# Nine loads that nobody reads, ahead of the first K tile of a decode attention kernel

## The chip, the cores and the metric

The kernel runs on one core of one Trainium2 chip. The metric is the device time of one execution in microseconds. Before the change the median of two runs is 1277.88 us (1277.71 to 1278.06).

## The reference

One token (a row `x` of 448 numbers) passes through two branches, which a gate mixes:

```
g = sigmoid(sum(x * gate_w))
q = x @ wq                                   # 16 heads of 256, two to a K/V head
p = softmax(q . k_cache / 16)                # 8 K/V heads, 65536 positions each
a = (p @ v_cache) @ wo                       # 4096 -> 448
b = (relu(x @ W_gate) * (x @ W_up)) @ W_down # 448 -> 1792 -> 448
out = g * a + (1 - g) * b
```

All inputs are bf16. The two caches, 8 x 65536 x 256 each, are nearly all of the data: 537 MB of the 549 MB that the kernel reads.

## The kernel before

**Tiles.** Each K/V head is cut into four tiles of 16384 positions (`NTH = 4`), 32 tiles of K and 32 of V. A tile is a `[128, 32768]` bf16 buffer: 128 partitions with 64 KB each. For K, a partition's 64 KB lie 256 KB after those of the partition before it in memory (`k_src`), for V 64 KB (`v_src`). There are three such buffers, `ring[0]` to `ring[2]`, which K and V tiles, and at the end the last pieces of V and `wo`, use in turn.

**What happens to a tile.** VectorE transposes a K tile in place in 32 x 32 blocks (L373, in two halves for the first head), TensorE forms the scores of both query heads (L388, L414), VectorE joins the two score banks and takes the maximum (L559, L561), ScalarE exponentiates (L563). After a head's fourth K tile VectorE rescales and transposes the probabilities (L580, L582), and TensorE multiplies them with the V tiles (L461, L414). A buffer is free again when TensorE has read it.

**Who issues the loads.** The list `order` names the loads in the order in which SyncE issues them, with due times; each operation carries a key (its due time), and each engine runs its operations in the order of their keys. SyncE issues nearly everything: first the main part of `wq` (key 3.0, into `ring[2]`), then `W_up` (3.002), the rest of `wq` (`wqa`, 3.01, into the first columns of `ring[1]`), K tile 0 (into `ring[0]`), eight small loads of 5 or 3 partitions that bring the last 64 rows of `W_gate` and `W_up` (`rows64`, L399), `W_down` (L539, which waits until `q` is formed, since it overwrites `wq`), K tile 1 (into `ring[1]`), K tiles 2 and 3, and from there V and K by turns. ScalarE issues `W_gate`, `x` and `gate_w` at the start. GpSimd issues no load before the change; it clears a part of `ring[2]` first (L257), for which `rows64` waits, and then makes identity matrices and selectors.

**When a tile's load may start.** `slot` gives each tile its buffer, `freed` what must be done with that buffer before, and `held` starts this record with what stands in the buffers at the beginning: `q` in buffer 1, the gate/up products and the down product in buffer 2. A name in it stands for the operation or the load of that name in `l_`, and `free()` turns it into a wait of the tile's load. The wait is made on a count: a DMA's semaphore has its full count when all its parts have landed.

**The end.** The last V tile comes in three pieces (L603), with pieces of `wo` (L618) behind them; two copies (L656) and a small store (L658) end the program.

Of the kernel before, what the change touches and what calls it, by code (L numbers as in the profile page):

```python
# [24 lines left out]
class _Plan:  # L25
# [13 lines left out]
    def dma(self, eng, key, sem, fn, deps=()):  # L39
        if sem not in self.dsem:  # L40
            self.dsem[sem] = self.es.enter_context(self.nc.semaphore("d_" + sem))
        o = _Op(eng, key, fn, deps, dma=sem)
        self.ops.append(o)
        return o
# [59 lines left out]
def bass_gated_mix__gqa_block_cached__glu_gated_reglu__decode_kernel(  # L104
# [39 lines left out]
    with es:  # L144
# [3 lines left out]
        ring = [sb("ring%d" % i, [128, U * DH], BF) for i in range(NRING)]  # L148
# [59 lines left out]
        op, dma = pl.op, pl.dma  # L208
# [30 lines left out]
        T_END = t + 20.0  # L239


        slot, held, freed = {}, {1: ["q"], 2: ["gu", "dn"]}, {}
        r = 0
        for kind, i, _ in order:
            if kind in ("k", "v") or (kind, i) in (("wo", 0), ("vp", 0)):
# [158 lines left out]
        l_, qk, smax, aexp, pv, last = {}, {}, {}, {}, {}, {}  # L404
# [83 lines left out]
        for kind, i, t in issue:  # L488
            if kind == "wq":
                l_["wq"] = dma("sp", t, "wq", lambda e: e.dma_start(wq3, A_wq[0:NR3, :].rearrange("(p k) n -> p (k n)", k=R3)))  # L490
                l_["wqh"] = dma("sp", t + 0.01, "wqh", lambda e: e.dma_start(
                    wqa, A_wq[NR3:D, :].rearrange("r (c n) -> (r c) n", c=2)))
                tq = tL["wq", 0]
# [54 lines left out]
            elif kind == "k":  # L548
                n = i
# [45 lines left out]
            elif kind in ("v", "vp"):  # L595
                if kind == "v":
                    n, lo, hi = i, 0, U
# [99 lines left out]
```

## Time and profile before

| | before |
|---|---|
| median of the runs | 1277.88 us (2 runs, 1277.71 to 1278.06) |
| the profiled execution | 1277.58 us |
| its span in the profile | 1276.3 us |
| busy: VectorE, TensorE, ScalarE, GpSimd | 685.0, 352.4, 51.2, 10.6 us |
| bytes moved by DMA | 549.46 MB, 431 GB/s over the span |
| SyncE's queue (with ScalarE's first loads in another) | 99.4% of 16 engines' span |

The span runs from the first to the last instruction of the profile; the profiled execution's own time is 1.28 us longer. Engines' busy times overlap, so they do not add up to the span. In the views of stretches each row gives a stretch of the span, its length, the busy time (and number) of each engine's instructions in it, TensorE's granted clock, the mean busy share of the 16 DMA engines and the rate. In the views of waits a row says which queue and line waited for what: us in total, times, longest. In the view of DMA issues the last number is the median time from issue to landing, where it is known. In a timeline a row begins with its start and its length in us.

### The profile page before, as it was taken

The numbers are of one execution on the slowest core, as the hardware profiler recorded it, in microseconds if no ns is written. First come the engines' busy times: TensorE is split into PE (matmuls) and PEld (weight loads), VectorE is DVE, ScalarE is ACT, GpSimd is POOL, SyncE is SP. The second block draws the span as 40 slices with busy tenths as digits, with TensorE's granted clock in tenths as the row PEclk, the third lists the DMA queues.
The fourth block names the chain that finished last, engine by engine and source line by source line (L and its number), as shares of the span: only waits on it lengthen the run. The fifth ranks groups of instructions, "written<-read, shape, count | busy, mean of one in ns | idle before, by whom it ended". The sixth has DMA issues, their size and how long they took to land.

```text
span 1276.3 us, 6848 instructions
## 1 busy us (share of the span) xinstructions
PE 352.4 (28%) x4447; PEld 70.6 (6%) x1875; DVE 685.0 (54%) x283; ACT 51.2 (4%) x84; POOL 10.6 (1%) x23
## 2 busy tenths in 40 slices
PE   3322323213122240133320242211323203223135
PEld 2000000000000000000000000000000000000001
DVE  2688733576534755445555454556535566336521
ACT  0000000000000000000000000000000000000000
POOL 3000000000000000000000000000000000000000
PEclk9556666665666565666655666656766556666567
DMA  9999999999999999999999999999999999999998
GB/s 403 439 434 429 440 430 429 438 431 434 433 426 444 433 428 433 430 442 430 428 438 431 430 435 430 432 440 433 430 432 432 440 431 430 432 435 440 426 421 368
DMA packets 11594, 549.46 MB, mean 431 GB/s; under 512 B 1287, under 2 KB 1418, under 8 KB 2570
## 3 DMA queue, kind: packets, MB, share of 16 engines
q1 hardware_dynamic: 11418, 547.66, 99.4%
q10 hardware_dynamic: 148, 1.38, 0.3%
q8 instruction: 24, 0.39, 0.1%
q14 instruction: 4, 0.03, 0.0%
HBM read 549.03 MB, written 0.00 MB: 430 GB/s over the span
## 4 chain that ended last, share of the span: by engine, by line
DVE 40%; DMA 28%; PE 17%; another core or an unknown queue 11%; ACT 1%; issue 1%; SPq 0%; ACTq 0%; DVEq 0%
DVE ring L373 32%; DMA ring<-in_A_k_cache_dram 24%; PE ST L388 5%; PE ST L414 5%; PE O L414 4%; DMA ring<-in_A_wo_dram 3%; PE O L461 2%; DVE o_sb L423 2%; DVE P L582 1%; DVE P L580 1%; ACT P L563 1%; DMA P<-in_A_x_dram 1%; DVE nmb L561 1%; DVE ST L559 1%
## 5 line engine op out<-in xcount | busy, mean ns | idle before, releaser
L373 DVE STREAM_TRANSPOSE ring<-ring 128x16384 uint32<-128x16384 uint32 (+1 forms) x36 | 552.3, 15346 | 311.6 <-DMA ring<-in_A_k_cache_dram 307.2
L388 PE MATMUL ST<-ring,xm 128*16 128x512 bf16 x1024 | 140.1, 539 | 772.5 <-DVE ring L373 772.5
L414 PE MATMUL ST<-ring,xm 128*16 128x512 bf16 x1024 | 137.1, 527 | 0.0
L414 PE MATMUL O<-ring,P 128*32 128x512 bf16 x1524 | 118.6, 423 | 0.0
L559 DVE COPY_PREDICATED ST<-bm,ST 128x512 f32<-128x512 uint16 x32 | 22.2, 694 | 168.7 <-PE ST L414 168.7
L563 ACT ACTIVATE P<-ST,nmb 128x512 bf16<-128x512 f32 x32 | 45.3, 1415 | 1135.8 <-DVE nmb L561 1135.8
L388 PEld LDWEIGHTS ST<-ring,xm 128*16 128x16 bf16 x1024 | 31.8, 115 | 929.1 <-DVE ring L373 801.1
L461 PE MATMUL O<-ring,P 128*32 128x512 bf16 (+1 forms) x524 | 56.3, 427 | 23.6 <-DMA ring<-in_A_v_cache_dram 23.5
L423 DVE CAST_PREDICATED o_sb<-bm,O 128x512 bf16<-128x512 uint16 (+1 forms) x33 | 22.3, 679 | 62.1 <-PE O L414 58.8
L580 DVE TENSOR_TENSOR P<-P,hs 128x2048 bf16<-128x2048 bf16 x8 | 18.3, 2293 | 8.5 <-ACT hs L577 8.5
L561 DVE TENSOR_REDUCE nmb<-ST 128x1 f32<-128x512 f32 x32 | 22.1, 691 | 1.1
L461 PEld LDWEIGHTS O<-ring,P 128*32 128x32 bf16 (+1 forms) x524 | 15.9, 113 | 119.8 <-issue 91.4
L582 DVE STREAM_TRANSPOSE P<-P 128x2048 bf16<-128x2048 bf16 x8 | 18.5, 2311 | 0.3
L587 PE MATMUL M_ps<-hs,ones_f 128*128 128x2 f32 x16 | 4.7, 363 | 46.0 <-DVE hs L586 46.0
L441 PE MATMUL M_ps<-emat,o_sb 128*128 128x2 bf16 x72 | 3.3, 167 | 23.6 <-DVE o_sb L433 23.2
L563 ACT ACTIVATION_READ_ACCUMULATOR P<-ST,nmb 128x1 f32 x32 | 8.5, 266 | 0.0
L339 PE MATMUL M_ps<-ring,P 128*128 128x256 bf16 x48 | 7.1, 321 | 0.3 <-DVE gb L295 0.3
L308 DVE COPY xm<-P 1x64 bf16<-1x64 bf16 x2 | 0.3, 190 | 12.2 <-DMA P<-in_A_x_dram 12.2
L587 PEld LDWEIGHTS M_ps<-hs,ones_f 128*128 128x128 f32 x16 | 4.0, 312 | 46.7 <-DVE hs L586 46.7
L573 PE MATMUL M_ps<-identf,hs 128*2 128x128 f32 x8 | 2.2, 270 | 15.8 <-DVE hs L571 15.8
L257 POOL MEMSET ring<- 64x7168 bf16 x1 | 6.1, 6064 | 0.3 <-POOLq L682 0.3
L481 DVE TENSOR_SCALAR attnT<-M_ps,hs 64x4 bf16<-64x4 f32 x16 | 3.5, 220 | 3.8 <-PE M_ps L441 3.7
(89 smaller groups left out, 79.8 us busy)
## 6 DMA issues: line engine op xcount, KB each, us to landing
ring<-in_A_v_cache_dram SPq DMA_DIRECT2D x1, 4096.0 KB, 29.8
ring<-in_A_v_cache_dram SPq DMA_DIRECT2D x2, 2048.0 KB, 36.5
ring<-in_A_wq_dram SPq DMA_DIRECT2D x1, 3072.0 KB, 13.2
ring<-in_A_wo_dram SPq DMA_DIRECT2D x4, 448.0 KB, 39.6
ring<-in_B_W_down_dram SPq DMA_DIRECT2D x1, 1568.0 KB, 17.1
ring<-in_B_W_gate_dram ACTq DMA_DIRECT2D x1, 1344.0 KB, 13.5
ring<-in_B_W_up_dram SPq DMA_DIRECT2D x1, 1344.0 KB, 16.0
ring<-in_A_wo_dram SPq DMA_DIRECT2D x1, 1344.0 KB, 18.7
```

The costliest lines, as they stand in the source:

```text
L339: ins = e.matmul(QN_ps, xw3[:, kt, 31 - j:159 - j], wq3[:, kt * NQ + j * 256:kt * NQ + (j + 1) * 256], start=(j == 0 and kt == 0), stop=Fa ...
L373: return lambda e: e.transpose(v, v)
L388: ins = e.matmul(o, xm[:, x0:x0 + 16], v, start=st, stop=False, skip_group_check=True, tile_position=(0, 32 * w))
L414: return e.add_instruction(mybir.InstMatmult(name=nc.get_next_instruction_name(), engine=e.engine, ins=[e.lower_ap(v), e.lower_ap(w, for_m ...
L423: return e.copy_predicated(dst, m.to_broadcast(list(src.shape)), src)
L461: ins = e.matmul(o, w, v, start=st, stop=False, skip_group_check=True, tile_position=(0, 32 * g))
L559: join = op("dv", tk + 25.2, lambda e: e.copy_predicated(ST[0][:], bm[:, NB:NB + 1].bitcast(mybir.dt.uint16).to_broadcast([128, 512]), ST[ ...
L561: smax[n] = op("dv", tk + 26, lambda e, n=n, NM=NM, t_=t_: e.tensor_reduce(NM[:, t_:t_ + 1], ST[0][:], AX.X, ALU.max, negate=True), [join, ...
L563: aexp[n] = op("ac", tk + 27, lambda e, n=n, t_=t_, NM=NM, RS=RS, Ph=Ph: e.activation(Ph[:, t_:2048:4], ST[0][:], ACTF.Exp, bias=NM[:, t_: ...
L580: rsc = op("dv", T + 16, lambda e, X=X, pb=pb: e.tensor_tensor(pb, pb, X[:, 12:16].unsqueeze(1).to_broadcast([128, 512, 4]), ALU.mult), [h ...
L582: last["ev", h] = [op("dv", T + 17, lambda e, Ph=Ph: e.transpose(Ph[:], Ph[:]), [rsc])]
L587: l3 = mop("pe", T + 19, lambda e, X=X: e.matmul(LS_ps, ones_f[:, :], X[:, 6:8], start=True, stop=True), [l2, c_one])
```

## The change

Nine loads of parts of `wq` are added, into columns of `ring[1]` (the buffer of K tile 1) that hold nothing else at that time. No instruction reads what they bring. Seven are issued by SyncE, with keys just behind the weights' and ahead of K tile 0's: load `i` takes `27 + 3 i` rows of `wq`, three rows (24 KB) to a partition, to the `9 + i` partitions `i`, `i + 8`, `i + 16`, ... Two are issued by GpSimd ahead of everything else that it does: four partitions each, 24 KB to a partition, 0, 8, 16, 24 and 32, 40, 48, 56. K tile 1, which overwrites the buffer, waits for them too. On the other engines no instruction is added, removed or moved.

```diff
-        slot, held, freed = {}, {1: ["q"], 2: ["gu", "dn"]}, {}
+        slot, held, freed = {}, {1: ["q", "pk", "pg"], 2: ["gu", "dn"]}, {}
...
                 l_["wq"] = dma("sp", t, "wq", lambda e: e.dma_start(wq3, A_wq[0:NR3, :].rearrange("(p k) n -> p (k n)", k=R3)))
+                for i in range(7):
+                    l_["pk"] = dma("sp", 3.02 + 0.001 * i, "pk", lambda e, i=i: e.dma_start(
+                        ring[1][i:i + 8 * i + 65:8, 8192:20480], A_wq[0:3 * i + 27, :].rearrange("(p k) n -> p (k n)", k=3)))
+                for i in range(2):
+                    l_["pg"] = dma("gp", -0.9 + 0.01 * i, "pg", lambda e, i=i: e.dma_start(
+                        ring[1][i * 32:i * 32 + 25:8, 20480:32768], A_wq[12 * i:12 * i + 12, :].rearrange("(p k) n -> p (k n)", k=3)))
                 l_["wqh"] = dma("sp", t + 0.01, "wqh", lambda e: e.dma_start(
                     wqa, A_wq[NR3:D, :].rearrange("r (c n) -> (r c) n", c=2)))
```

## The prediction

> **What bounds the kernel now.** I read the page's header first, then the busy time by stretches of the span, then the waits of SyncE's queue.
>
> ```profile
> span 1276.3 us, 6848 instructions
> DMA packets 11594, 549.46 MB, mean 431 GB/s; under 512 B 1287, under 2 KB 1418, under 8 KB 2570
> core 0: us, PE busy (x) PEld busy (x) DVE busy (x) ACT busy (x) POOL busy (x), PEclk, DMA share, GB/s
> 64.31:103.00 38.69, 6.64 (x68) 1.10 (x32) 35.67 (x8) 2.79 (x4) 0.00 (x0) 0.57 1.00 434
> 200.00:400.00 200.00, 57.05 (x765) 9.48 (x285) 104.22 (x35) 9.00 (x14) 0.00 (x0) 0.63 1.00 433
> 400.00:800.00 400.00, 103.02 (x1319) 18.75 (x519) 214.64 (x81) 15.56 (x26) 0.00 (x0) 0.63 1.00 433
> 1200.00:1240.00 40.00, 17.27 (x221) 4.16 (x93) 12.95 (x14) 1.85 (x4) 0.00 (x0) 0.67 0.97 413
> ```
>
> From 200 to 800 us the sixteen DMA engines are busy all the time (share 1.00) and move 433 GB/s, while VectorE is busy about half and TensorE a quarter. One engine thus moves 433 / 16 = 27.06 GB/s. All bytes at that rate take 549.46 / 0.433 = 1269.0 us, against the execution's 1277.58: the transfers set the time, and only 8.6 us, at the two ends, is not theirs. That is also all that any edit that removes no bytes could win at this rate.
>
> ```profile
> SPq L599 <- PE ST L414: 905.8, 29, 36.1
> SPq L552 <- PE O L414: 165.0, 27, 15.4
> ring<-in_A_k_cache_dram SPq DMA_DIRECT2D x32, 50.4
> ring<-in_A_v_cache_dram SPq DMA_DIRECT2D x31, 35.0
> ```
>
> SyncE waits nearly always for a free ring buffer, but ahead of need. A tile is 128 x 64 KB = 8.39 MB, or 19.4 us at 433 GB/s; a K tile lands 50.4 us and a V tile 35.0 us after its issue (medians), so 31 and 15.6 us of other work lie queued ahead of them. Late issues start to cost only once these are used up.
>
> **Few partitions, few engines.** Whether a load of 9 partitions is shared by all engines decides its price, and before has such loads: L399 brings eight of 5 or 3 partitions, between the first K tile and W_down.
>
> ```profile
> ring<-in_B_W_gate_dram SPq DMA_DIRECT2D x2, 70.0 KB
> ring<-in_B_W_gate_dram SPq DMA_DIRECT2D x1, 52.5 KB
> ring<-in_B_W_gate_dram SPq DMA_DIRECT2D x1, 31.5 KB
> ring<-in_B_W_up_dram SPq DMA_DIRECT2D x2, 70.0 KB
> ring<-in_B_W_up_dram SPq DMA_DIRECT2D x1, 52.5 KB
> ring<-in_B_W_up_dram SPq DMA_DIRECT2D x1, 31.5 KB
> ring<-in_B_W_down_dram SPq DMA_DIRECT2D x1, 1568.0 KB, 17.1
> 37.85 8.71 DVE L373 STREAM_TRANSPOSE ring<-ring 128x8192 uint32<-128x8192 uint32 x1 [7.32 <-DMA ring<-in_A_k_cache_dram]
> 41.29 1.67 PE L526 MATMUL O<-ring,xT 20*1 20x448 bf16 x32 [11.53 <-DMA ring<-in_B_W_up_dram]
> 28.22 36.09 DMA ring<-in_A_k_cache_dram
> ```
>
> K tile 0 releases VectorE at 37.85; K tile 1 (the last row, from the chain of waits: issued at 28.22) lands 36.09 us later, at 64.31. In these 26.46 us lie the tile (19.37 us), W_down (1.606 MB, 3.71 us) and the eight loads, gate and up, 448 KB in all. What remains for these is 26.46 - 23.08 = 3.38 us. Spread over 16 engines they would take 0.459 MB / 433 GB/s = 1.06 us. On as many engines as partitions, the fullest engine has 2 x (14 + 14 + 10.5 + 10.5) = 98 KB, 3.71 us at 27.06 GB/s. The measured 3.38 us lies there, and it was paid in full by the next tile: a lag of a few engines holds up everybody, because a tile is complete with its last engine. So I count the new loads by their fullest engine.
>
> **The change, part by part.** It removes nothing. It adds nine DMA issues and, for K tile 1, a wait for them.
>
> *Seven loads of SyncE*, 9 to 15 partitions, 24 KB each, queued behind the weights and ahead of K tile 0. Load i has 9 + i partitions; if each goes to one engine, counted from the first, nine engines get seven packets each, the tenth six, the sixteenth none. A packet is 24,576 B / 27.06 GB/s = 0.908 us. Lower bound: each engine at full rate, 7 x 0.908 = 6.36 us. Upper bound: here the destination partitions step by eight (0, 8, ... 64 in the first), while L399's step by four (0, 4, ... 16). [...] I take the upper end, since the rows nearest to the limit show no part of the reading side: K tiles alone, whose rows lie 256 KB apart, come at 434 GB/s (64.31 to 103.00), K and V by turns, V's rows 64 KB apart, at 433. What is read does not set the rate, and where it is written may.
>
> [...]
>
> *Two loads of GpSimd*, 4 partitions each (0, 8, 16, 24 and 32, 40, 48, 56), at the start, beside the weights. One packet on an engine is 0.91 us; if both loads end in the same four sets, 1.82 us. No row shows a GpSimd load. I take the middle, 1.3 us; a gain is excluded because all engines are loaded at that time:
>
> ```profile
> 0.00:20.00 20.00, 2.22 (x18) 1.70 (x19) 4.93 (x25) 1.49 (x2) 10.64 (x23) 1.00 0.97 400
> 0.73 6.06 POOL L257 MEMSET ring<- 64x7168 bf16 x1 [0.29 <-POOLq L682]
> 1.65 0.43 SPq L491 DMA_DIRECT2D ring<-in_A_wq_dram  x1
> 2.12 0.54 SPq L552 DMA_DIRECT2D ring<-in_A_k_cache_dram  x1
> 6.82 3.01 SPq L399 DMA_DIRECT2D ring<-in_B_W_gate_dram  x4
> 9.87 2.85 SPq L399 DMA_DIRECT2D ring<-in_B_W_up_dram  x4
> 20.72 0.16 DVE L322 TENSOR_REDUCE emat<-identb 128x4 bf16<-128x64 bf16 x1
> 27.82 0.35 SPq L539 DMA_DIRECT2D ring<-in_B_W_down_dram  x1
> ring<-in_A_wq_dram SPq DMA_DIRECT2D x1, 512.0 KB, 16.8
> ```
>
> *Issue time: 0 us.* Seven more issues at 0.54 to 0.75 us (3.01 / 4) push K tile 0's issue from 2.12 to about 6 or 7.5 us, under weights that land until about 18.4 (the second part of wq: issued at 1.65, 16.8 us to landing). GpSimd's two issues stand before the 6.06 us memset for which L399 waits; from 0.4 to 3 us each, they move it to at most 13 and L399's last issue to about 19, with K tile 0 in the queue until 37.85 or later; identb, which VectorE reads at 20.72, also stays ahead. Without that cover they would cost 6 us.
>
> *The new wait: 0 us.* K tile 1 writes over the padding, so SyncE now waits for it: 18.4 + 14.0 = 32.4 us instead of 28.22. Behind it in SyncE's queue stand K tiles 2 and 3, which wait for later things. K tile 0, by then landing at about 51.9, hides these 4 us; they would be paid only if it did not.
>
> *What is late next.* K tile 0 lands 14 us later and so does every tile behind it, on the loaded engines; VectorE, TensorE and the ring follow their last engine, so the depth of 15.6 us is the same for that engine. The others run ahead and idle, which costs nothing.
>
> Sum: 12.7 + 1.3 = 14.0 us. 1277.58 + 14.0 = 1291.6 for the profiled execution; the median of the runs is 0.3 above it, which gives **1291.9 us**, 1.1% slower.
>
> **The rivals.**
>
> *Engines at full rate, no sharing:* 6.36 + 0.91 = 7.3 us, 1285.2. For it: L399's loads ran at full rate. Against it: their partitions do not collide.
>
> *Spread or hidden:* over all engines 92 packets of 24,576 B are 2.26 MB / 433 GB/s = 5.2 us, 1283.1; if the engines with the loads are not the ones that end last, down to 0, 1277.9. Against it the 3.38 us above.
>
> *Not slower: engines out of step read faster.* [...] The best of the page's 40 slices shows 444 GB/s:
>
> ```profile
> GB/s 403 439 434 429 440 430 429 438 431 434 433 426 444 433 428 433 430 442 430 428 438 431 430 435 430 432 440 433 430 432 432 440 431 430 432 435 440 426 421 368
> ```
>
> All along, that gives (549.46 + 2.26) / 0.444 + 8.6 = 1251 us. Against it: the engines are already 3.38 us apart from L399, and wide stretches hold 433. [...]
>
> *Slower by much: the skew eats the ring.* 14.0 + 3.4 = 17.4 us between first and last engine is more than the 15.6 us queued ahead of a V tile. If the late engine were not the same in each tile, every V tile would lose 17.4 - 15.6 = 1.8 us, 31 x 1.8 = 56 us: 1348. It decides from a skew above 15.6. Against it: the late engines stay the same, and only the early ones run dry; the stretch from 1200 to 1240 (0.97) is the one place where queues run short now.
>
> **How the numbers follow.** Chances: forecast 0.60; full rate 0.27; spread or hidden 0.07; out of step 0.02; skew 0.04. The range runs from the spread case, 1283.0, to the forecast with each bound at its top (12.7 + 1.8 = 14.5, 1292.4) and some 2.6 us for a late weight or a second packet on one engine (3 x 0.9): 1295.0. It leaves out the skew, the gain, fully hidden loads and a little of the forecast. The forecast's own range is 1289 to 1295. Two per cent (25.6 us) is about what a measurement of this kernel can tell from no change. Only the skew (0.04) lies above, and about half of the gain's chance below; the rest, 0.95, is within.
>
> **What would show it.** Right: K tile 0 releases VectorE at about 52 instead of 37.85, K tile 1 lands near 78; the wide stretches stay at 433 GB/s or a little less where early engines idle; the end moves by as much as K tile 1. A shift of 7 us says full rate, 5 us evenly spread, and one that shrinks on the way says that the ring gave it back. Wrong altogether: a steady rate away from 433, or a shift that grows from tile to tile.

## The result and the profile after

The changed kernel takes 1295.19 us (1295.15 to 1295.23, two runs) against 1277.88 before: 17.3 us more, a ratio of 1.0137 (95% interval 1.012 to 1.0153). That is slower, as forecast, by less than two per cent, and 0.2 us above the upper end of the forecast's range (1295.0).

The rate by slices, from the page of the kernel after:

```profile
GB/s 308 414 426 430 434 430 436 434 432 434 434 428 438 432 432 434 434 434 432 432 434 432 432 434 434 436 430 434 434 428 434 438 432 434 430 436 432 432 394 363
```

The first slice has fallen from 403 to 308 GB/s, the second from 439 to 414; from the third on all is as it was. The view of stretches says where (the last three numbers of a row are the clock, the DMA share and the rate):

```profile
20.00:30.00 10.00, 8.12 (x52) 6.23 (x53) 3.76 (x14) 0.20 (x1) 0.00 (x0) 1.00 1.08 244
400.00:800.00 400.00, 104.85 (x1351) 19.11 (x539) 223.76 (x82) 15.57 (x26) 0.00 (x0) 0.62 1.00 433
```

Between 20 and 30 us, while the padding is loaded, the engines count as busy all the time and move little more than half of 433 GB/s (244): each packet takes longer. By the trace's records of single packets, those of the seven loads (24,576 B) that start in this stretch take 1.80 us (median), where packets of the same size in the kernel before take 0.91; those of K tile 0 (65,536 B) take 3.98 to 4.99 us instead of 2.42. Later the rate is the old one. How the delay travels (timeline, chain of waits, waits of SyncE's queue, DMA issues of the kernel after; the last two rows are the chain of waits of the kernel before):

```profile
55.23 8.71 DVE L373 STREAM_TRANSPOSE ring<-ring 128x8192 uint32<-128x8192 uint32 x1 [20.75 <-DMA ring<-in_A_k_cache_dram]
7.08 29.04 DMA ring<-in_A_wq_dram
82.14 8.71 DVE ring L373
1250.47 41.26 DMA ring<-in_A_wo_dram
SPq L558 <- DMA ring<-in_A_wq_dram: 3.9, 1, 3.9
ring<-in_A_k_cache_dram SPq DMA_DIRECT2D x32, 50.3
ring<-in_A_v_cache_dram SPq DMA_DIRECT2D x31, 35.0
...
64.34 8.71 DVE ring L373
1233.24 40.82 DMA ring<-in_A_wo_dram
```

K tile 0 releases VectorE at 55.23 instead of 37.85 (17.4 us later), K tile 1 at 82.14 instead of 64.34 (17.8), and the last piece of `wo` has landed at 1291.73 instead of 1274.06 (17.7). The whole loss is there at K tile 0; nothing is added or given back after K tile 1. The last padding lands at 36.12 (issued at 7.08, 29.04 us), and SyncE waits 3.9 us for it before K tile 1. This should cost nothing, since K tile 0 is on its way until 55.23; that was not tried by itself. K and V tiles land as long after their issue as before.

### The profile page after: what moved, and what is told of

The parts are those of the page before. It is cut to its first block, busy times and chain, and to the rows that moved or that the text cites. A ratio compares the mean times of both kernels' runs of the same rounds, so it can differ in the third digit from the quotient of the medians.

```text
span 1293.9 us, 6857 instructions
## 1 busy us (share of the span) xinstructions
PE 353.8 (27%) x4446; PEld 70.7 (5%) x1875; DVE 684.9 (53%) x283; ACT 51.2 (4%) x84; POOL 12.0 (1%) x25
## 3 DMA queue, kind: packets, MB, share of 16 engines
q10 hardware_dynamic: 148, 1.38, 0.3%
## 4 chain that ended last, share of the span: by engine, by line
DVE 39%; DMA 30%; PE 17%; another core or an unknown queue 11%; ACT 1%; issue 1%; SPq 1%; DVEq 0%
DVE ring L373 32%; DMA ring<-in_A_k_cache_dram 24%; PE ST L388 5%; PE ST L414 5%; PE O L414 4%; DMA ring<-in_A_wo_dram 3%; DMA ring<-in_A_wq_dram 2%; PE O L461 2%; DVE o_sb L423 2%; DVE P L588 1%; DVE P L586 1%; ACT P L569 1%; DVE nmb L567 1%; DVE ST L565 1%
## 5 line engine op out<-in xcount | busy, mean ns | idle before, releaser
L373 DVE STREAM_TRANSPOSE ring<-ring 128x16384 uint32<-128x16384 uint32 (+1 forms) x36 | 552.3, 15345 | 325.3 <-DMA ring<-in_A_k_cache_dram 320.9
L257 POOL MEMSET ring<- 64x7168 bf16 x1 | 6.1, 6096 | 0.0
## 6 DMA issues: line engine op xcount, KB each, us to landing
ring<-in_A_wq_dram SPq DMA_DIRECT2D x1, 3072.0 KB, 16.4
ring<-in_B_W_gate_dram ACTq DMA_DIRECT2D x1, 1344.0 KB, 16.6
```

Source lines behind the costliest of these rows:

```text
L373: return lambda e: e.transpose(v, v)
```

## The experiments

Each kernel was timed beside the kernel before on the same chip (its medians there 1277.76 to 1277.93); differences are between medians. All of them are below two per cent; one is told as a difference where the interval of its ratio does not reach 1.

**Which half costs what.** One half of the change left out, then GpSimd's two loads with less data, then issued by SyncE. In each kernel `held` names only the loads that are left.

```diff
# sp_only: the change without
-                for i in range(2):
-                    l_["pg"] = dma("gp", ...)
# gp_only: the change without
-                for i in range(7):
-                    l_["pk"] = dma("sp", ...)
# gp_tiny: gp_only with
-                        ring[1][i * 32:i * 32 + 25:8, 20480:32768], A_wq[12 * i:12 * i + 12, :].rearrange("(p k) n -> p (k n)", k=3)))
+                        ring[1][i * 32:i * 32 + 25:8, 20480:20736], A_wq[4 * i:4 * i + 4, 0:256]))
# gp_by_sync: gp_only with
-                    l_["pg"] = dma("gp", -0.9 + 0.01 * i, ...
+                    l_["pg"] = dma("sp", 3.0001 + 0.0001 * i, ...
```

> SyncE's seven loads alone, without GpSimd's two. Theory A (two engines share one way in, 14 packet times of 0.908 us, as forecast; GpSimd's loads were the term set too low): +12.7 to +13.5 us against the kernel before, VectorE released by K tile 0 at 51 instead of 37.85. Theory B (GpSimd's loads cost the 1.3 us of the forecast, and the seven cost more than forecast, because K tile 0 collides with the padding too): +16.

> GpSimd's two loads alone. Theory A: each holds up all 16 engines for about 0.85 us (the rate falls for all in the stretches in which they run), and both lay one packet on the same four engines: 1.7 + 1.8 = +3.5 us. Theory B: +1.3 us. Taken by their bytes alone: +0.5 us.

> GpSimd's two loads alone, with 512 B instead of 24 KB to a partition (4 KB in all). Theory A: what holds up all engines comes with the load and not with its bytes: +1.7 us. If the cost goes by the bytes: 0.

> The same two loads of 4 partitions, issued by SyncE between the first weight and the second. Theory A: no stop of all engines, two packets on the first four engines, partly in one another's way: +1.8 to +3.6 us, and the other twelve engines hardly late. If it is the few partitions alone that made GpSimd's loads dear, as much as with GpSimd.

Measured: `sp_only` 1290.89 us, +13.1 (ratio 1.0105, 1.009 to 1.012), VectorE released at 51.27. `gp_only` 1281.14, +3.3 (1.0027, 1.0017 to 1.0037). `gp_tiny` 1277.90, +0.1 (1.0001, 0.9992 to 1.0011). `gp_by_sync` 1281.11, +3.3 (1.0027, 1.0017 to 1.0037).

So the seven loads cost what was forecast, and theory B falls. GpSimd's two cost 3.3 us, not 1.3. But theory A's reason for it, that a load of GpSimd stops all engines, falls too: loads with 4 KB in all cost nothing, and SyncE's cost the same as GpSimd's. It is their bytes, and where they go.

**Where the bytes are written, or where they are read.** Seven loads of eight partitions, eight apart; the same four apart; eight apart from another source; and 2.10 MB spread evenly, about as much as the change's own seven loads bring (2.06 MB; seven loads of eight partitions bring 1.38 MB).

```diff
# eight_step8: sp_only with
-                        ring[1][i:i + 8 * i + 65:8, 8192:20480], A_wq[0:3 * i + 27, :].rearrange(...)
+                        ring[1][i:i + 57:8, 8192:20480], A_wq[0:24, :].rearrange(...)
# eight_step4: eight_step8 with
+                        ring[1][i % 4 + 32 * (i // 4):i % 4 + 32 * (i // 4) + 29:4, 8192:20480], A_wq[0:24, :].rearrange(...)
# eight_step8_far: eight_step8 with
+                        ring[1][i:i + 57:8, 8192:20480], k_src(8 + i)[0:8, 0:12288]))
# even128: one load instead of the seven
+                l_["pk"] = dma("sp", 3.02, "pk", lambda e: e.dma_start(
+                    ring[1][:, 8192:16384], A_wq[0:NR3, :].rearrange("(p k) n -> p (k n)", k=R3)[:, 0:8192]))
```

> [...] Theory A2 (where two engines write into one set of partitions, every engine falls to half its rate): 7 x 1.82 = +12.7 us. Rival S (the loads are slow because all of them read the same 192 KB of wq): also about +12.7. Without either: +6.4.

> The same seven loads, same source, with the eight partitions four apart (0, 4, ... 28 and so on), so that no two of a load lie in one set. Theory A2: full rate, 7 x 0.91 = +6.4 us. Rival S: as with partitions eight apart, about +12.7.

> The seven loads of eight partitions eight apart again, reading eight rows of seven other K tiles, 256 KB apart, instead of the one place in wq. Theory A2: as from wq, +12.7 us. Rival S: full rate, +6.4.

> One load of 128 partitions with 16 KB each, 2.10 MB, about as many bytes as SyncE's seven loads (2.06 MB). All theories: every engine gets eight pieces of 16 KB, 2.10 MB / 433 GB/s = +4.8 us. Should the last engines of before have room to spare, less.

Measured: `eight_step8` 1290.64 us, +12.85 (1.0101, 1.0086 to 1.0116); `eight_step4` 1284.24, +6.45 (1.0051, 1.0036 to 1.0066); `eight_step8_far` 1290.85, +13.1 (1.0103, 1.0088 to 1.0118); `even128` 1282.70, +4.9 (1.0039, 1.0025 to 1.0053). The first two differ in nothing but the numbers of the partitions written; a slowing of this kind is called a collision below. Another source changes nothing that can be told (0.2 us). The rival S falls. The rows of the stretch from 20 to 30 us of `eight_step8`, `eight_step8_far` and `eight_step4`, in this order:

```profile
20.00:30.00 10.00, 9.48 (x83) 6.50 (x69) 2.38 (x12) 0.37 (x1) 0.00 (x0) 1.00 0.95 203
...
20.00:30.00 10.00, 9.48 (x74) 6.82 (x67) 2.26 (x10) 0.37 (x1) 0.00 (x0) 1.00 0.94 216
...
20.00:30.00 10.00, 9.48 (x86) 6.69 (x72) 2.84 (x14) 0.37 (x1) 0.00 (x0) 1.00 1.07 461
```

With partitions eight apart the rate of all sixteen engines together falls to 203 GB/s, less than half of 461. (Rates of short stretches are rough: a packet counts whole where it starts, as busy shares above 1.00 show.) If only the engines of the eight partitions, taken as eight, ran at half rate, it would be 8 x 13.5 + 8 x 27.06 = 325 GB/s. So by this estimate the other eight, which load K tile 0 at that time, are slowed as well.

The traces keep a record of every packet, which the views only sum up, and these records show it directly. In `eight_step4` a packet of the seven loads (24,576 B) takes 0.91 us and a packet of K tile 0 (65,536 B) 2.42 us. In `eight_step8` a packet of the seven loads takes 1.89 us (median), and the first 24 packets of K tile 0 take 4.4 to 4.9 us. That would be three for each of eight engines: K tile 0 stands behind the seven loads in SyncE's queue, so the author takes it that engines without a part in the collisions carry it meanwhile. Which engine carries a packet was not shown.

**GpSimd's term.** The two loads of four partitions, four apart: by SyncE, by GpSimd, and in the whole change.

```diff
# four_step4: gp_by_sync; gp_step4: gp_only; after_gp4: the change; each with
-                        ring[1][i * 32:i * 32 + 25:8, 20480:32768], ...
+                        ring[1][i * 32:i * 32 + 13:4, 20480:32768], ...
```

> The two loads of four partitions issued by SyncE, now to partitions four apart (0, 4, 8, 12 and 32, 36, 40, 44), so that each of the first four engines writes into a set of its own. Theory A2: two packets at full rate on four engines, +1.8 us, and the other twelve engines keep their rate. If loads of few partitions cost more for another reason, +3.3 as with partitions eight apart.

> GpSimd's two loads alone, to partitions four apart. Theory A2: +1.8 us, nothing being special about GpSimd's loads. If a part of their +3.3 us is GpSimd's own, more than with SyncE.

> The whole change, with GpSimd's two loads to partitions four apart. Theory A2: 13.1 us of the seven loads and 1.8 of GpSimd's = +14.9; what the whole change has beyond the sum of its parts (17.3 against 13.1 + 3.3) stays, +15.8, if it belongs to the late engines, and goes if it belongs to the collisions of GpSimd's loads.

Measured: `four_step4` 1279.53 us, +1.8 (1.0014, 1.0005 to 1.0023); `gp_step4` 1279.29, +1.5 (1.0012, 1.0003 to 1.0021); `after_gp4` 1293.26, +15.5 (1.0121, 1.0106 to 1.0137). With partitions four apart the two packets cost 1.8 us at most, whoever issues them; the runs of `gp_step4` (1278.92 to 1279.89 us) and `gp_only` (1280.93 to 1281.76) do not overlap, nor do those of `four_step4` and `gp_by_sync`. `after_gp4` lies between its two expectations, 14.9 and 15.8. The stretch in which SyncE's two loads run, in `gp_by_sync` and in `four_step4`:

```profile
14.00:17.00 3.00, 0.21 (x8) 0.22 (x9) 0.65 (x6) 0.00 (x0) 0.00 (x0) 1.00 0.97 209
...
14.00:17.00 3.00, 0.40 (x9) 0.32 (x9) 1.60 (x10) 0.00 (x0) 0.00 (x0) 1.00 0.96 405
```

Two loads of four partitions each run beside the weights, and all sixteen engines together move 209 instead of 405 GB/s. The records of single packets agree. GpSimd's eight packets take 0.91 us each in `gp_step4`, but 1.15 to 1.22 and 1.40 to 1.45 us in `gp_only`; SyncE's take 0.91 us in `four_step4`, but 1.12 to 1.31 and 1.87 to 1.89 in `gp_by_sync`, where packets of 10,752 B of the weights beside them take up to 0.86 us instead of 0.40.

The weights go to all 128 partitions, so the loads four apart are written beside the same weights, and nothing slows (405 GB/s, 0.91 us a packet). Why eight apart slows them and four apart does not is not shown: no view tells which engine writes which partitions.

**What is left over.** 13.1 + 3.3 are 16.4 us, the change costs 17.3. GpSimd's two loads were added to the seven of eight partitions.

```diff
# eight_step4_gp and eight_step8_gp: eight_step4 and eight_step8 with the change's
+                for i in range(2):
+                    l_["pg"] = dma("gp", ...)
```

> SyncE's seven loads of eight partitions four apart (alone +6.45 us) with GpSimd's two as in the change (alone +3.3). Theory L (the 0.9 us beyond the sum come from late engines that prolong the collisions in SyncE's loads): no collisions there, so the plain sum, +9.8. Rival R (the two kinds of loads together cost 0.9 more wherever they write): +10.7.

> SyncE's seven loads of eight partitions eight apart (alone +12.85 us) with GpSimd's two. Both theories: the sum 16.2 and 0.9 more, +17.1. If it is only the plain sum, the 0.9 belong to the engines from the ninth on, which the change loads and this kernel does not.

Measured: `eight_step4_gp` 1287.51 us, +9.6 (1.0075, 1.0061 to 1.0088); `eight_step8_gp` 1294.51, +16.6 (1.0129, 1.0115 to 1.0143). Without collisions among the seven there is nothing beyond the sum (9.75), which speaks against R. With them (`eight_step8_gp`) there is 0.4 us at the end, where both theories gave 0.9, and more at K tile 0. The releases of VectorE by K tile 0 in `eight_step8`, `gp_only` and `eight_step8_gp`:

```profile
50.82 8.71 DVE L373 STREAM_TRANSPOSE ring<-ring 128x8192 uint32<-128x8192 uint32 x1 [19.84 <-DMA ring<-in_A_k_cache_dram]
...
41.02 8.71 DVE L373 STREAM_TRANSPOSE ring<-ring 128x8192 uint32<-128x8192 uint32 x1 [7.14 <-DMA ring<-in_A_k_cache_dram]
...
55.44 8.71 DVE L373 STREAM_TRANSPOSE ring<-ring 128x8192 uint32<-128x8192 uint32 x1 [21.18 <-DMA ring<-in_A_k_cache_dram]
```

Against 37.85 these are 13.0, 3.2 and 17.6 us: 1.4 more than the sum. `after_gp4`, whose GpSimd loads do not collide, is 0.9 us above the sum of its parts too (15.5 against 13.1 and the 1.5 of `gp_step4`), so the surplus does not need collisions of GpSimd's loads. The rest goes with collisions among late engines, theory L, as far as these runs say; its size is not settled, and differences of half a microsecond are near what the medians repeat to.

**A lag that before pays itself.** The prediction read 3.38 us for the eight small loads of L399. `tail_even` spreads them; GpSimd's clearing (L257), for which they waited, is left out with them.

```diff
-            for c, (n, m, r0) in enumerate(((5, 4, 0), (5, 4, 20), (5, 3, 40), (3, 3, 55))):
-                p0 = 32 * i_ + c
-                d_ = dma("sp", t + 0.0001 * c, sem, ... wfh[p0:p0 + 4 * n - 3:4, 0:m * F], ...
+            d_ = dma("sp", t, sem, lambda e: e.dma_start(
+                wfa[i_], W[NR3:D, :].rearrange("r (c n) -> (r c) n", c=2)))
...
-                    for b in range(4):
+                    for c in range(2):
...
+                            for w in range(2 * c, 2 * c + 2):
+                                ins = e.matmul(OP[i_][32 * w:32 * w + 1, 0:FW], xT[:, R3 + c:R3 + c + 1],
+                                               wfa[i_][:, (w - 2 * c) * FW:(w - 2 * c + 1) * FW], ...
```

> The kernel before, without any added load, with the last 64 rows of W_gate and W_up brought by one load of 128 partitions each (half a row to a partition) instead of eight loads of 5 or 3 partitions, and the products formed from them in eight instead of 32 matmuls. By the 3.38 us that the eight loads were read to cost, against 0.459 MB / 433 GB/s = 1.06 us spread evenly: -2.3 us, 1275.5. If the few engines that they load are not those that end last: 0.

Measured: 1278.86 us, 1.1 more than before (1.0009, 1.0001 to 1.0018). K tiles 0 and 1 in its timeline (L372 is L373 here), and SyncE's issue of the last two whole V tiles but one in it and in the kernel before:

```profile
37.99 8.71 DVE L372 STREAM_TRANSPOSE ring<-ring 128x8192 uint32<-128x8192 uint32 x1 [6.86 <-DMA ring<-in_A_k_cache_dram]
63.61 8.71 DVE L372 STREAM_TRANSPOSE ring<-ring 128x8192 uint32<-128x8192 uint32 x1 [4.95 <-DMA ring<-in_A_k_cache_dram]
1174.17 3.79 SPq L594 DMA_DIRECT2D ring<-in_A_v_cache_dram  x2
...
1173.10 3.78 SPq L599 DMA_DIRECT2D ring<-in_A_v_cache_dram  x2
```

From tile 0 to tile 1 it takes 25.62 us instead of 26.49: 0.9 won where 2.3 were expected, and at 1174 us it is 1.1 behind. Both expectations miss. Something makes single engines late on the way by a microsecond or two, and in the kernel before the few engines loaded by L399 seem not to be the ones that it hits. That is argued, not shown; the cause stays open. No version beat the kernel before.

## Why the prediction was right, and where it was not

**Right.** The bound: with 433 GB/s in the middle before and after, only work put in front moves the end, and the end moved by nearly as much as K tile 0 (17.7 and 17.4 us). Counting by the fullest engine and not by bytes: about 2.1 MB cost 4.9 us spread evenly and 13.1 as seven loads, of which each engine's packets explain 6.4 (`eight_step4`) and the collisions the other half (`eight_step8`). SyncE's term, 12.7 us, measured 13.1. The choice between its two ends, for which no row of before spoke clearly, was a bet that the runs bear out in its price: with the eight partitions of a load eight apart a packet takes 1.89 us, with four apart 0.91, and the seven loads 12.85 and 6.45 us. The 12.7 us are seven packets of an engine at half rate, 7 x 1.82. That two engines share one way in, or that partitions form sets, as theories A and A2 have it, no run shows; the runs show these times by the step between the partitions, in their place.

**Wrong, the step that failed: GpSimd's two loads, 1.3 us.** They measure 3.3. The prediction took them to lay one or two packets on an engine at full rate, 0.91 to 1.82 us. The reckoning behind SyncE's 12.7 us, half rate for each packet, was left out here, although the weights were being written all the while. In the runs the two loads slow themselves and the weights: their packets take 1.15 to 1.45 us in `gp_only` instead of 0.91, and the weights' packets beside them take longer too. With partitions four apart the same loads cost 1.5 to 1.8. Half rate for both packets, 2 x 1.82 = 3.6 us, would have been near the measured price, though no packet of GpSimd's was slowed that much; with it the sum would have been 16.3 us, and 1294.2 the forecast. Of the 3.3 us between the sum of 14.0 and the measured 17.3, GpSimd's loads are 2.0, SyncE's 0.4, and the remaining 0.9 is the interplay of the two groups, which no term of the sum stood for and whose cause is argued, not shown.

**Wrong in the mechanism, though not in its price.** The prediction reckoned the loaded engines at half rate and let the others "run ahead and idle". In the runs all engines slow down: 203 GB/s where 325 would be left. In `eight_step8` K tile 0's first 24 packets took 4.4 to 4.9 us instead of 2.42. The time came out the same by luck, because the late engines set the end and each of their packets took twice as long either way (1.89 us). Why the other engines slow as well is not shown.

**Wrong, a reading.** "A lag of a few engines holds up everybody" was read from the 3.38 us behind L399 as a cost of the whole run. `tail_even` does not win it back. Even spread evenly, 25.62 - 23.08 = 2.5 us remain for these loads up to K tile 1 where 1.06 were reckoned, so about 1.5 of the 3.38 us were no lag of a few engines. For the added loads counting by the fullest engine held, as `eight_step4` shows (6.45 us for seven packets). The remark that a measurement can tell about two per cent was too coarse as well: the runs of one kernel here lie within 1.3 us, a tenth of a per cent.

**The rivals.** Full rate for all is what `eight_step4` does, not the change. Spread evenly is `even128`. Hidden loads, engines out of step reading faster, and skew eating the ring did not occur: K and V tiles land 50.3 and 35.0 us after issue, and 433 GB/s hold. Since all engines slowed together, the skew was probably also smaller than the 17.4 us of that rival; it was not measured. The nine issues and the new wait of 3.9 us stayed covered, as far as the sums tell; for GpSimd's two issues `gp_tiny` shows it (0.1 us).

## What to carry to other kernels

In a kernel bound by its transfers, price a load of few partitions by the fullest DMA engine, and look at which partitions it writes: here partitions eight apart about halved the rate of everything in flight, against four apart, from 461 to 203 GB/s in loads of eight and from 405 to 209 in loads of four beside the weights. Four apart instead of eight took the same seven loads from 12.85 to 6.45 us, and spread over all 128 partitions half as many bytes again cost 4.9. A small saving on a few engines is worth trying but not worth believing: it may not be those that end last.

## What the hardware showed unexpectedly

A collision slows, with one engine reckoned to a partition, engines that have no part in it: two loads of four partitions eight apart brought all sixteen engines from 405 to 209 GB/s, and in `eight_step8` packets of K tile 0 took 4.4 to 4.9 us instead of 2.42. GpSimd's loads cost as much as SyncE's of the same shape (3.3 and 3.3 us; 1.5 and 1.8 without collisions), and 4 KB of them cost nothing measurable beside full queues (0.1 us).
